# Attention backward with a period of eight half-steps, and a share of the base values made in the channel loop

## The chip, the core and the metric

The kernel runs on one core of one Trainium2 chip. The metric is the device time of one launch, in microseconds, median of several runs. A core has five engines with a queue each, and every queue is worked off in order: TensorE (PE, matrix products, results in PSUM), VectorE (DVE), ScalarE (ACT), GpSimd (POOL) and SyncE (SP, which here only issues transfers). They wait for one another through semaphores.

## What is computed

The launch computes a forward pass and all its gradients. The output mixes an attention block and a state-space block with a gate of one value for each token:

```python
g = _sigmoid((x * gate_w).sum(-1, keepdims=True))
a = _A_ref(x, A_wqkv, A_wo)          # 32 heads of width 18, 2048 tokens, width 576
b = _B_ref(x, B_A_re, ..., B_Dskip)  # a long convolution for each of 576 channels, 128 states
return g * a + (1 - g) * b
...
scores = jnp.einsum("bhqd,bhkd->bhqk", q, k) * (Dh ** -0.5)
p = _softmax(scores, axis=-1)
o = jnp.einsum("bhqk,bhkd->bhqd", p, v)
...
P = jnp.exp(logdA[:, :, None] * l[None, None, :])
K = jnp.einsum("dn,dnl,dn->dl", Cc, P, dB).real
```

`reference` returns the output and, by `jax.vjp`, the gradients of twelve inputs.

## The kernel before

The program has four stages. The first one (s1) projects x to q, k and v, makes the gradient of the attention's output and prepares parameters. The second one is the attention, forward and backward. The third (s4) loops over 18 blocks of 32 channels for the state-space part. The last one makes the weight gradients and the outputs. The change concerns the second and the third.

**Attention.** Heads are taken in 8 groups of four (`NG`), and each group's queries in 4 pieces of 512 tokens (`NQ`). A pair of group g and piece b is a *unit*; there are 32 (`NU`). The four heads of a group lie in four strips of 32 partitions, so that products over two heads run side by side in TensorE. A unit is worked off in 32 *half-steps* (`NST`), so 1024 in all (`NTOT`), and one loop over G runs through them with the order of every engine written out by hand (`manual_schedule`: nothing is reordered). In half-step G

- the forward part of half-step G makes the scores of two heads for 128 keys and 512 queries (`P1`, PSUM tile `ps` of tag S), and ScalarE their exponential `PT` (L802, 128x1024);
- the backward part runs 39 half-steps behind (`OFF`, G2 = G - 39). It makes the same scores the other way round (`P3`, tag S as well, exponential `eb`, L807) and the products of dO and V for two heads (`P2`, tag dP, two buffers of one bank). VectorE multiplies each of these with `PT` into `ds` (L812, 128x512), two for each half-step.

Tag S has two buffers of two banks, used in turn by P1 and P3, so P1 of the next half-step can be written only when the exponential of this P1 has been read. PSUM has one bank more for `accO` (the forward result) and one single bank of tag `accB`. Everything else shares `accB`, one after the other:

- V: eight products `accV<-eb,dOa` for the gradient of v (`dv_burst`, evicted by VectorE at L502 or L508);
- Q: eight products `accQ<-ds,Ktok` for the gradient of q (`dq_burst`, L523 or L528);
- K: sixteen half-width products `accK<-dsT,Qtok` for the gradient of k (`dk_half` twice, L554 or L556), which need `ds` transposed (`dsT`);
- F: once in a unit the transposition of the forward result (L411).

These bursts come with a period of four half-steps: V, Q, K and a fourth one, in which TensorE turns one head's part of `ds` (`turn_ds`, four 128x128 transpositions into `dst_p`, L463, copied by VectorE to `dsT`, L464). The other head parts are turned by transfers that SP issues (L820): of the eight head parts of a pair of key blocks, seven by transfer and one by TensorE, and all eight by transfer in one pair of eight (`by_pe`). `fill` puts products of two constant tiles into the bank ahead of the real ones; `NFILL` says how many: none for V and Q, one for K, three in the fourth half-step. A half-step's burst is called after the next half-step's P1 (`evs = late()`).

`post_forward` ends a unit's forward part: `f0` copies `accO` (L407); `f1` turns it and VectorE scales it (L416, L419), GpSimd makes `dOa` and `prod` (L421, L423); `f2` reduces `prod` (L429) and SP turns `dOa` into `dOaT`, which P2 of that unit reads.

**Base values.** The s4 stage needs for every channel a table E of powers (128 x 2 x 128). In the attention GpSimd, otherwise little used, makes it: 36 groups (`k`) of 16 channels, each with 28 small instructions that make powers and then 48 of 256 elements (`e_main`, L571: 32 products `et<-eG,eT` and 16 sums `Eo<-et,et`), and a store to memory for every four channels (`E_d<-Eo`, L619). `e_emit` spreads them over the half-steps by an estimate of their cost. GpSimd's queue also holds the packing of finished gradients (`pack`, L446 and L447, six half-steps after the transfer that turns them) and, at each unit's end, L421 and L423.

**The channel loop (s4).** For each block i: VectorE's recurrence (`scan`, 14 steps of L997, L1000, L1001), its products L1016, L1022, L1023, then `pairs1` and `pairs2` (L1067, L1095), all on two operands in SBUF. TensorE's products with `E1n` (loaded from `E_d` by `load_en`, six buffers) and with its transposed copy `E1e` stand around them. GpSimd has two small instructions for each block (`sums`, L1103 and L1104), which read `m4`, a copy that ScalarE makes into a single buffer (L1101).

Of the kernel before, what the change touches and what calls it, by code (L numbers as in the profile page):

```python
# [17 lines left out]
P = 128  # L18


def build(tc, aps, dbg_aps=None, stages=("s1", "attn", "post", "s4", "final")):
# [40 lines left out]
    with ExitStack() as gctx:  # L62
# [275 lines left out]
        x_v = x2.rearrange("(t p) d -> p t d", p=P)  # L338
        if "attn" in stages:
# [4 lines left out]
            NFILL = (0, 0, 1, 3)  # L344
            with ExitStack() as ctx:
                ctx.enter_context(tc.manual_schedule(engines={mybir.EngineType.PE, mybir.EngineType.Activation, mybir.EngineType.DVE, mybir.EngineType.Pool, mybir.EngineType.SP}))
                ga = ctx.enter_context(tc.tile_pool(name="ga", bufs=2))
                ptp = ctx.enter_context(tc.tile_pool(name="ptp", bufs=21))
# [39 lines left out]
                PB = {"QaT": 3, "VaT": 4, "Vtok": 5, "Ktok": 4, "Qtok": 2}  # L388
# [4 lines left out]
                def new_unit(g, b):  # L393
                    U = dict(PT={}, ds={}, eb={})
                    U["dO"] = work.tile([P, TPQ, 4, DH], BF, tag="dO", name="dO_b")
                    nc.sync.dma_start(U["dO"].rearrange("p t a b -> p t (a b)"),
                                      dO_d[:, b * TPQ:(b + 1) * TPQ, 4 * g * DH:4 * (g + 1) * DH])
                    U["dOa"] = dOa2[(g * NQ + b) % 2]
                    UN[(g, b)] = U

                def post_forward(g, b, acc):
# [7 lines left out]
                    def f1(po):  # L409
# [4 lines left out]
                        def ev():  # L414
# [7 lines left out]
                            prod = st["prod"] = work.tile([P, TPQ, 4, DH], F32, tag="prod", bufs=1, name="prod")  # L422
# [13 lines left out]
                def grad_tile():  # L436
                    return work.tile([P, KB], BF, tag="gb", bufs=3, name="gb")

                def store_grad(gb, g, which, t0):
                    c0 = which * D + g * 4 * DH  # L440
                    gT = work.tile([P, TPQ, 4, HP], BF, tag="gT", bufs=3, name="gT")
                    nc.sync.dma_start_transpose(out=gT.rearrange("p t a b -> p t (a b)"), in_=gb)

                    def pack():
                        dtk = work.tile([P, TPQ, 4, DH], BF, tag="dtk", bufs=2, name="dtk")
                        nc.gpsimd.tensor_copy(dtk, gT[:, :, :, 0:DH])  # L446
                        nc.gpsimd.dma_start(dqkv_d[:, t0:t0 + TPQ, c0:c0 + 4 * DH], dtk.rearrange("p t a b -> p t (a b)"))  # L447
                    packs.append((now[0] + 6, pack))
# [9 lines left out]

                def turn_ds(U, p):

                    pt_ = apsp.tile([P, TPQ, P], BF, tag="accB", name="dst_p")
                    for qb in range(TPQ):
                        nc.tensor.transpose(pt_[:, qb, :], U["ds"][2 * p + 1][:, 0, qb * P:(qb + 1) * P], ident_bf)  # L463
                    return lambda: nc.vector.tensor_copy(U["dsT", p][:, 1, 0:TPQ, :], pt_)  # L464

                def by_pe(g, b, p):
                    return ((g * NQ + b) * (NST // 4) + p) % 8 != 5

# [13 lines left out]
                ACC = []  # L482
# [7 lines left out]
                def dv_burst(g, b, kq, half):  # L490
                    U = UN[(g, b)]
                    acc = ACC.pop()
                    for n_ in range(2):
                        ii = 2 * half + n_
                        for j in range(4):
                            mm(acc[HP * j:HP * (j + 1), :], lhsT=U["dOa"][:, ii, j, :], rhs=U["eb"].pop((kq, ii, j)),
                               start=(n_ == 0), stop=(n_ == 1), tile_position=(0, HP * j))

                    def ev():
                        if b == 0 and half == 0:  # L500
# [3 lines left out]
                        a_ = DKV[("v", g, kq)]  # L504
                        o_ = a_
                        if b == NQ - 1 and half == 1:
                            o_ = DKV[("v", g, kq)] = grad_tile()
# [3 lines left out]
                def dq_burst(g, b, p):  # L511
                    U = UN[(g, b)]
                    acc = ACC.pop()
                    for n_ in range(2):
                        i = 2 * p + n_
                        for j in range(4):
                            mm(acc[HP * j:HP * (j + 1), :], lhsT=grp_t[g]["Ktok", i // TPQ][:, i % TPQ, HS * j:HS * j + HP], rhs=U["ds"][i][:, j, :],
                               start=(n_ == 0), stop=(n_ == 1), tile_position=(0, HP * j))

                    def ev():  # L520
                        if p == 0:
# [4 lines left out]
                        if p == NST // 4 - 1:  # L526
# [4 lines left out]
                def dk_half(g, b, p, h, st):  # L531
                    U = UN[(g, b)]
                    if h == 0:
                        st["acc"] = ACC.pop()
                    acc = st["acc"]
                    for qb in (2 * h, 2 * h + 1):
                        for j in range(4):
                            mm(acc[HP * j:HP * (j + 1), 0:2 * P].rearrange("p (a b) -> p a b", b=P), lhsT=grp_t[g]["Qtok", b][:, qb, HP * j:HP * (j + 1)],
                               rhs=U["dsT", p][:, :, j * TPQ + qb, :], start=(qb == 0), stop=(qb == 3), tile_position=(0, HP * j))
                    if h == 0:  # L540
                        return None
                    kq = p // 2
                    sl = slice((p % 2) * 2 * P, (p % 2 + 1) * 2 * P)

                    def ev():
                        if b == 0 and p % 2 == 0:
                            DKV[("k", g, kq)] = work.tile([P, KB], F32, tag="dkacc", bufs=4, name="dkacc")
                        a_ = o_ = DKV[("k", g, kq)]
                        if b == NQ - 1:
                            if p % 2 == 0:  # L550
                                DKV[("kb", g, kq)] = grad_tile()
                            o_ = DKV[("kb", g, kq)]
                        if b == 0:
                            nc.vector.tensor_copy(a_[:, sl], acc[:, 0:2 * P])  # L554
                        else:
                            nc.vector.tensor_tensor(o_[:, sl], a_[:, sl], acc[:, 0:2 * P], op=A.add)  # L556
                    return ev

                CE = 16
                EH = 4  # L560
                NA, NBT = P // 16, 16
                T_ = work.tile([P, 2, CE, NBT + 1], F32, tag="eT", bufs=1, name="eT")
                G_ = work.tile([P, 2, CE, NA], F32, tag="eG", bufs=1, name="eG")
                for t_ in (T_, G_):
                    nc.gpsimd.memset(t_[:, 0, :, 0], 1.0)
                    nc.gpsimd.memset(t_[:, 1, :, 0], 0.0)
                eops = []
                ez = {}

                def pl(out, a, b, op):  # L570
                    nc.gpsimd.tensor_tensor(out, a, b, op=op)  # L571

                def e_tmp(k):
                    return work.tile([P, 2 * P], F32, tag=f"et{k}", bufs=1, name=f"et{k}")

                def load_z(k):
                    ez[k] = work.tile([P, 2, CE], F32, tag="ez", bufs=2, name="ez")
                    nc.gpsimd.dma_start(ez[k], par_d[:, 12:14, k * CE:(k + 1) * CE])

                def emit_power(dst, src, lo, n, sq):  # L580

                    x = src[:, :, :, 1:1 + n]
                    st = []

                    def mul(ri):
                        w_ = e_tmp(ri)[:, 0:2 * CE * n].rearrange("p (r c m) -> p r c m", r=2, c=CE)
                        pl(w_, x, sq[:, ri].unsqueeze(1).unsqueeze(3).to_broadcast([P, 2, CE, n]), A.mult)
                        st.append(w_)
                    est = 0.21 + 2 * CE * n * 0.0018
                    eops.append((est, lambda: mul(0)))  # L590
                    eops.append((est, lambda: mul(1)))
                    est = 0.2 + CE * n * 0.002
                    eops.append((est, lambda: pl(dst[:, 0, :, lo:lo + n], st[0][:, 0], st[1][:, 1], A.subtract)))
                    eops.append((est, lambda: pl(dst[:, 1, :, lo:lo + n], st[0][:, 1], st[1][:, 0], A.add)))

                Eo = {}

                def e_main(k, c):
                    q = k * CE + c
                    for ri in range(2):  # L600
                        st = []

                        def mul(gi, ti, st):
                            if ti == gi == 0 and q % EH == 0:
                                Eo[q // EH] = work.tile([P, EH, 2, P], BF, tag="Eo", bufs=2, name="Eo")
                            w_ = e_tmp(gi)
                            pl(w_.rearrange("p (c a b) -> p c a b", c=2, b=NBT),
                               G_[:, gi, c:c + 2, :].unsqueeze(3).to_broadcast([P, 2, NA, NBT]),
                               T_[:, ti, c:c + 2, 0:NBT].unsqueeze(2).to_broadcast([P, 2, NA, NBT]), A.mult)
                            st.append(w_.rearrange("p (c l) -> p c l", c=2))  # L610

                        def add(ri, st):
                            o_ = Eo[q // EH][:, q % EH:q % EH + 2, ri, :]
                            if ri == 0:
# [827 lines left out]
```

## Time and profile before

| | us |
|---|---|
| median of 3 runs | 3099.37 (3094.06 to 3100.29) |
| profiled execution | 3094.2, span 3092.5 |
| s1 | 0 to 206 |
| attention, forward only (39 half-steps) | 206 to 248 |
| attention, both parts | 248 to 2219 |
| attention, backward only (the last 39 half-steps and their bursts) | 2219 to 2302 |
| s4: preparation and first blocks | 2302 to 2360 |
| s4: the rest of the loop | 2360 to 2880 |
| last stage | 2880 to 3092.5 |

The stages' borders are first and last starts of `PT`, `eb` and of the recurrence. The page's sums over the whole span put PE at 84% of it, DVE at 80%, ACT at 77% and POOL at 58%. No engine stands out there, and these shares are means over stages that differ: POOL is busy almost only in the attention. So the stages are read one by one.

### The profile page before, as it was taken

What the parts mean: (1) busy time and instruction counts of PE and PEld (TensorE: products, weight loads), DVE (VectorE), ACT (ScalarE), POOL (GpSimd) and SP (SyncE); (2) the same over time, 40 slices, a digit from 0 to 9 for tenths busy, and PEclk for the clock granted to TensorE, in tenths of its full rate; (3) what the DMA queues carried; (4) which work ended last, traced back from release to release, by engine and by line L of the source; (5) the groups of instructions that cost most, each with busy time, mean ns of one, the idle gap of its engine ahead of it and who ended that gap; (6) DMA issues with size and microseconds to landing.
All of it is one profiled execution on the core that took longest, in us unless ns stands there. A gap on an engine that the chain in (4) does not pass through costs nothing. (4 is left out here: it accounts for less than half of the span.)

```text
span 3092.5 us, 70491 instructions
## 1 busy us (share of the span) xinstructions
PE 2608.6 (84%) x27147; PEld 1202.5 (39%) x27147; DVE 2464.7 (80%) x4531; ACT 2395.3 (77%) x2765; POOL 1799.7 (58%) x3371
## 2 busy tenths in 40 slices
PE   4768999899899899889889989989866887786679
PEld 2432232232233233223223323323225777776347
DVE  4436898898899899889889989989964888888634
ACT  2458999999899899999899989989836677675111
POOL 0038888988888889888898888988110000000010
PEclk8878999999999899999999999999987888888789
DMA  8757999899989999989998998898788887772885
GB/s 221 154 142 129 173 165 180 156 168 166 163 166 164 170 163 165 178 158 167 164 165 163 172 171 159 167 172 162 133 151 243 213 208 204 206 200 79 228 205 132
DMA packets 1409063, 529.41 MB, mean 171 GB/s; under 512 B 1303487, under 2 KB 1378849, under 8 KB 1399509
## 3 DMA queue, kind: packets, MB, share of 16 engines
q1 hardware_dynamic: 1380212, 464.27, 78.5%
q0 software_dynamic: 20624, 53.26, 6.6%
q10 hardware_dynamic: 7888, 7.38, 0.8%
q8 instruction: 212, 3.47, 0.4%
q14 instruction: 127, 1.03, 0.1%
HBM read 144.48 MB, written 99.69 MB: 79 GB/s over the span
## 5 line engine op out<-in xcount | busy, mean ns | idle before, releaser
L812 DVE TENSOR_TENSOR ds<-ps_P,PT 128x512 bf16<-128x512 f32 x2048 | 1312.3, 681 | 18.5 <-PE ps_P L30 14.4
L807 ACT ACTIVATE eb<-ps_P 128x1024 bf16<-128x1024 f32 x1024 | 1058.1, 1033 | 125.1 <-PE ps_P L30 120.7
L802 ACT ACTIVATE PT<-ps_P 128x1024 bf16<-128x1024 f32 x1024 | 1058.7, 1037 | 41.1 <-PE ps_P L30 39.1
L571 POOL TENSOR_TENSOR et<-eG,eT 128x256 f32<-128x256 f32 x1152 | 700.1, 629 | 35.5
L30 PE MATMUL ps_P<-dOaT,VaT_g 32*128 32x512 bf16 x2048 | 561.9, 390 | 51.3 <-DVE ds L812 43.8
L30 PE MATMUL ps_P<-QaT_g,KaT_g 32*128 32x512 bf16 x2048 | 413.6, 398 | 124.7 <-ACT PT L802 110.0
L571 POOL TENSOR_TENSOR Eo<-et,et 128x256 bf16<-128x256 f32 x576 | 418.7, 727 | 42.4
L30 PE MATMUL ps_P<-KaT_g,QaT_g 32*128 32x512 bf16 x2048 | 406.2, 389 | 1.4 <-ACT eb L807 1.0
L1103 POOL TENSOR_TENSOR SS<-m 128x96 f32<-128x96 f32 x18 | 7.8, 431 | 556.9 <-ACT m L1101 556.9
L30 PEld LDWEIGHTS <-KaT_g 32*128 32x128 bf16 x2048 | 135.4, 92 | 432.7 <-issue 430.9
L30 PEld LDWEIGHTS <-QaT_g 32*128 32x128 bf16 x2048 | 114.9, 91 | 310.4 <-issue 288.3
L30 PE MATMUL accF<-ident_bf,J_bf 128*128 128x512 bf16 x783 | 225.8, 399 | 10.0 <-DVE gb L556 10.0
L30 PE MATMUL accO<-PT,Vtok_g 128*32 128x512 bf16 x2048 | 213.2, 403 | 0.0
L464 DVE COPY dsT<-dst_p 128x512 bf16<-128x512 bf16 x224 | 95.0, 424 | 111.0 <-PE dst_p L463 109.9
L30 PEld LDWEIGHTS <-J_bf 128*128 128x128 bf16 x1103 | 89.1, 100 | 226.3 <-issue 194.6
L30 PE MATMUL accK<-dsT,Qtok_g 128*32 128x256 bf16 x4096 | 166.0, 284 | 0.0
L30 PE MATMUL accQ<-ds,Ktok_g 128*32 128x512 bf16 x2048 | 158.9, 387 | 2.8 <-DVE gb L508 1.5
L30 PE MATMUL accV<-eb,dOa 128*32 128x512 bf16 x2048 | 159.0, 388 | 2.2 <-DVE dsT L464 1.6
L959 ACT COPY E1e<-etp 128x1024 bf16<-128x1024 bf16 x144 | 135.8, 1040 | 16.8 <-PE etp L958 16.8
L30 PE MATMUL yp<-Rw,E1n 128*128 128x30 bf16 x1152 | 67.7, 232 | 83.7 <-DVE Rw L1022 69.1
L30 PEld LDWEIGHTS <-E1n 128*128 128x128 bf16 x2304 | 96.7, 109 | 101.2 <-issue 100.7
L508 DVE TENSOR_TENSOR dvacc<-dvacc,accV 128x512 f32<-128x512 f32 x192 | 130.1, 678 | 0.1
(243 smaller groups left out, 3911.6 us busy)
## 6 DMA issues: line engine op xcount, KB each, us to landing
E_d<-Eo POOLq DMA_DIRECT2D x144, 256.0 KB, 3.9
E1n<-E_d SPq DMA_DIRECT2D x36, 1024.0 KB
xs<-xb_d SPq DMA_DIRECT2D x18, 1024.0 KB
T0w<-Kp_d SPq DMA_DIRECT2D x18, 1024.0 KB
Md_d<-mst SPq DMA_DIRECT2D x36, 288.0 KB
dsT<-ds SPq DMA_TRANSPOSE x512
dqkv_d<-dtk POOLq DMA_DIRECT2D x96, 72.0 KB, 4.4
QKV_d<-stg SPq DMA_DIRECT2D x12, 504.0 KB
```

Source lines behind the costliest of these rows:

```text
L30: return nc.tensor.matmul(out, lhsT=lhsT, rhs=rhs, start=start, stop=stop, **kw)
L464: return lambda: nc.vector.tensor_copy(U["dsT", p][:, 1, 0:TPQ, :], pt_)
L508: nc.vector.tensor_tensor(o_, a_, acc, op=A.add)
L571: nc.gpsimd.tensor_tensor(out, a, b, op=op)
L802: nc.scalar.activation(U["PT"][i][:, j:j + 2, :], ps, ACT.Exp)
L807: nc.scalar.activation(e, ps, ACT.Exp)
L812: nc.vector.tensor_tensor(U["ds"][i][:, j, :], ps, U["PT"][i][:, j, :], op=A.mult)
L959: nc.scalar.copy(E_[:, 4 * q:4 * q + 4], pt_)
L1103: nc.gpsimd.tensor_tensor(o_[:, :, 0], m4[:, :, 0], m4[:, :, 3], op=A.subtract)
```

## The change

- The bursts get a period of eight half-steps, set by `slot = (G2 + 1) % 8`: V in slots 0 and 1, Q in 2 and 3, K in 5 and 6. Two bursts now add up in the bank, and VectorE evicts once, after the second: 128x512 for V, Q and K alike. In slots 4 and 7 TensorE turns.
- A turn takes two head parts, the last head's of both key blocks of a pair (eight transpositions, one copy 128x2x512); one pair of eight is left to the transfers, the one whose slot F takes. Transfers turn three heads of each key block.
- `NFILL` becomes one fill for V and none elsewhere; the fourth half-step's three and K's one go.
- A burst is now issued in its own half-step, and V's second half comes one half-step after the last exponential that it reads. The heads of P2 and P3 are taken in another order, still in strips apart from each other.
- `PT` is held in 41 half tiles in place of 21 whole ones, `eb` has 8 buffers for 6, `ds` 5 for 4. Fewer: `Vtok` 4 for 5, `gb` and `gT` 2 for 3, `dtk` 1 for 2, `dO_b` 1 for 2 and loaded six half-steps later, `prod` shares a buffer with `oT`. Finished gradients are packed 4 half-steps after their transfer is issued.
- `basis_ops` makes the base values; groups 0 to 27 (`KE` = 28) stay in the attention, 28 to 35 are made in s4: `basis_share(i)` issues them in 15 equal shares from block -1 to block 13, ahead of `pairs2(i)` and `sums(i)` in the code, on GpSimd.
- `E1n` has 5 buffers for 6. The second half of block i+2 is loaded in the middle of block i; before, it was loaded with the first half, at the end of block i-1.

```diff
-            NFILL = (0, 0, 1, 3)
+            NFILL = {"V": 1, "Q": 0, "K": 0}
...
-                def by_pe(g, b, p):
-                    return ((g * NQ + b) * (NST // 4) + p) % 8 != 5
+                def by_pe(p):
+                    return 0 if p == NPF else NTURN
...
+                    n = by_pe(p)
+                    pt_ = apsp.tile([P, n, TPQ, P], BF, tag="accB", name="dst_p")
+                    for x in range(n):
+                        for qb in range(TPQ):
+                            nc.tensor.transpose(pt_[:, x, qb, :], U["ds"][2 * p + 2 - n + x][:, 3, qb * P:(qb + 1) * P], ident_bf)
+                    return lambda: nc.vector.tensor_copy(U["dsT", p][:, 2 - n:2, 3 * TPQ:, :], pt_)
+                NTURN, NPF = 2, 5
...
+                def dv_half(g, b, kq, h, acc):
+                    for ii in (2 * h, 2 * h + 1):
                         for j in range(4):
                             mm(acc[HP * j:HP * (j + 1), :], lhsT=U["dOa"][:, ii, j, :], rhs=U["eb"].pop((kq, ii, j)),
-                               start=(n_ == 0), stop=(n_ == 1), tile_position=(0, HP * j))
+                               start=(ii == 0), stop=(ii == 3), tile_position=(0, HP * j))
...
+                SLOTS = {0: ("V", dv_half, 0), 1: ("V", dv_half, 1), 2: ("Q", dq_half, 0), 3: ("Q", dq_half, 1), 5: ("K", dk_half, 0), 6: ("K", dk_half, 1)}
...
-                    evs = late()
+                    evs = []
+                    slot = (G2 + 1) % 8
+                    m_ = (G2 - (7, 8, 8, 8, 8, 8, 8, 0)[slot]) // 8
+                    if ("f1", G) in todo:
+                        acc = accB("accF")
+                        evs.append(todo.pop(("f1", G))[0](acc))
+                    elif 0 <= m_ < NTOT // 8:
...
+                            if h == 0:
+                                acc = accB("acc" + nm)
+                                fill(acc, NFILL[nm])
+                                burst(g, b, kq, 0, acc)
+                            else:
+                                evs.append(burst(g, b, kq, 1, acc))
...
+                        elif by_pe(2 * kq + (slot == 4)):
+                            evs.append(turn_ds(UN[(g, b)], 2 * kq + (slot == 4)))
...
-                for k in range(D // CE):
+            for k in range(k0, k1):
...
+                eops4, load_z4 = basis_ops(pw, KE, D // CE)
+                load_z4()
+                def basis_share(i):
+                    want = len(eops4) * min(1.0, (i + 2) / (NBLK - 3))
+                    while e4[0] < want:
+                        eops4[e4[0]][1]()
+                        e4[0] += 1
...
                         ybp(i, 0)
+                        if sb is not None:
+                            load_en(sb, 1)
                         ybp(i, 1)
...
-                        load_en(mb, 1)
...
+                    basis_share(i)
                     if cur:
                         pairs2(i)
                         sums(i)
```

## The prediction

> **What bounds the kernel now.** I read the busy sums by stage first, then the waits inside the long stage, then single half-steps, then the one place in s4 where GpSimd works. By stage (us; busy us and count of PE, its weight loads, DVE, ACT, POOL; granted clock, DMA share, GB/s):
>
> ```profile
> 206.00:248.20 42.20, 34.17 (x155) 7.86 (x155) 2.06 (x5) 37.77 (x40) 36.07 (x67) 0.50 0.18 41
> 248.20:2219.20 1971.00, 1789.54 (x17665) 589.56 (x17665) 1739.93 (x3066) 1840.56 (x1969) 1709.24 (x3185) 0.97 0.94 165
> 2219.20:2302.00 82.80, 65.97 (x624) 21.20 (x622) 72.71 (x131) 41.98 (x42) 11.79 (x20) 0.94 0.84 146
> 2360.00:2880.00 520.00, 401.53 (x6679) 380.77 (x6679) 446.83 (x912) 349.75 (x514) 15.72 (x36) 0.82 0.70 181
> ```
>
> In the attention four engines are busy 87 to 93%: none has the stage to itself, they hold each other up. In s4 DVE leads (447 of 520) and POOL does nothing. The waits between 300 and 2219 (total, times, longest, us) and ACT's and PE's timeline (start, us) over one period:
>
> ```profile
> PE ps_P L30 <- ACT PT L802: 98.2, 366, 0.5
> ACT eb L807 <- PE ps_P L30: 88.1, 232, 4.4
> DVE dsT L464 <- PE dst_p L463: 104.6, 207, 1.2
> DVE dl L429 <- POOL prod L423: 31.2, 12, 4.2
> ```
>
> ```profile
> 1230.89 1.04 ACT L802 ACTIVATE PT<-ps_P 128x1024 bf16<-128x1024 f32 x1
> 1231.79 1.06 ACT L807 ACTIVATE eb<-ps_P 128x1024 bf16<-128x1024 f32 x1
> 1232.69 1.07 ACT L802 ACTIVATE PT<-ps_P 128x1024 bf16<-128x1024 f32 x1
> 1234.59 1.02 ACT L802 ACTIVATE PT<-ps_P 128x1024 bf16<-128x1024 f32 x1
> 1235.83 1.02 ACT L807 ACTIVATE eb<-ps_P 128x1024 bf16<-128x1024 f32 x1 [0.22 <-PE ps_P L30]
> 1236.74 1.02 ACT L802 ACTIVATE PT<-ps_P 128x1024 bf16<-128x1024 f32 x1
> ...
> 1233.82 0.39 PE L30 MATMUL ps_P<-QaT_g,KaT_g 32*128 32x512 bf16 x2 [0.24 <-ACT PT L802]
> 1234.14 0.82 PE L30 MATMUL accF<-ident_bf,J_bf 128*128 128x512 bf16 x3
> 1235.02 0.38 PE L463 MATMUL dst_p<-ident_bf,ds 128*128 128x128 bf16 x4
> 1235.34 0.39 PE L30 MATMUL ps_P<-KaT_g,QaT_g 32*128 32x512 bf16 x2
> ```
>
> Unhindered exponentials start 0.90 us apart, so ACT's floor is 1.81 us a half-step, though each lasts 1.04. PT starts 1.80, 1.90, 2.15 apart, and 1.81 in the V half-step that follows: 7.66 for four, 1.915 each. The long one is the half-step with fills: between P1 (1233.82) and P3 (1235.34) PE does three fills (0.88) and four turns (0.32), and `eb` waits for P3. K's, with one fill (0.32) and 0.55 of products, loses 0.09. V and Q (0.59) lose nothing. Hence a burst of about 0.8 us hides under an exponential, and each 0.1 more costs 0.1.
>
> The stage needs 1971.0/984 = 2.003 a half-step, so 87 us are lost outside this pattern. They lie at unit ends, where `prod` is late on GpSimd (last wait above), and after each such stall the clock drops for 3.4 or 6.8 us.
>
> In s4 all DVE operands are in SBUF. POOL and DVE at the first `sums`:
>
> ```profile
> 2394.61 0.40 POOL L1103 TENSOR_TENSOR SS<-m 128x96 f32<-128x96 f32 x1 [88.12 <-ACT m L1101]
> 2394.98 0.45 POOL L1104 TENSOR_TENSOR SS<-m 128x96 f32<-128x96 f32 x1
> ...
> 2394.79 0.37 DVE L1001 TENSOR_TENSOR HG<-tz 128x128 f32<-128x128 f32 x1
> 2395.20 0.51 DVE L997 TENSOR_TENSOR tz<-HG,par 128x256 f32<-128x256 f32 x1
> 2395.74 0.29 DVE L1000 TENSOR_TENSOR tz<-tz,UV 128x128 f32<-128x128 f32 x1
> ```
>
> L1001 takes 0.29 alone (its median; the line after it, L1000, is back to its own 0.29) and 0.37 beside POOL, L997 0.43 and 0.51. Over the 17 such pairs that meet the recurrence, DVE's instructions took 3.55 us more than their medians for 15.0 us of POOL: 24%.
>
> [...]L1001 lay wholly beside POOL and lost 0.08, not 0.4. [...]
>
> **The change, part by part.**
>
> *Regular half-steps.* For eight: fills go from eight (six at 0.29, two at 0.32) to one, turns from eight to sixteen at 0.08. Bursts per slot become: V 0.91 with its fill; V again 0.59, but its last four products read an `eb` exponential from the half-step before, which ends some 0.3 after they could start, so about 0.89; Q 0.59 twice; turn 0.64; K 0.55 twice; turn 0.64. Only the two V slots pass 0.8: together 0.08 to 0.24, I take 0.16. Eight cost 8 x 1.81 + 0.16 = 14.64 against 15.32: 0.085 a half-step, over 984: **-84 us**.
>
> *DVE.* Evictions fall from 2.4 for V and Q and 0.7 for K to 1.8 (0.60 from start to start). A turn's copy doubles from 0.42[...]; I take 0.7. Per eight, DVE goes from 13.9 to about 13.2, 90% of 14.64. As ACT sets the pace this is worth nothing by itself. The 0.51 us wait for `dst_p` goes with the fills: turns end where `ds` ends.
>
> *Unit ends.* GpSimd is busy 1709 of 1971 there. A group of base values is 42.2 us (L571 1435.9 and L619 84.7 us, over 36), so eight are 338 us; what stays is 1371 of some 1840, 75%. The lateness of `prod` should go. Its packs come 4 half-steps after their transfer, with one `dtk`; the 25% of slack covers that. I leave 0.6 us a unit for F and 20 us for clock dips, 39 of the 87: **-48 us**.
>
> *Tail.* DVE is busy 72.7 of 82.8; with its fewer evictions and no fills: **-8 us**. The first half-steps start at clock 0.50[...]: **+5**.
>
> *Transfers.* `dsT` moves 50 head parts for 57 in a unit, so DMA (share 0.94) is not fuller at the faster pace. K's second half reads `dsT` six half-steps (11 us) after its issue, not seven; transfers issued at 1231.30 had moved by 1237, so nothing is due. SP's loads that move (`Vtok` two later, `dO_b` six later) are needed 18 and 28 half-steps on. Two `gb` for three may hold K's eviction in the last unit of a group, by 1 us at most: 0 to 30 us, I take 0.
>
> *s4.* Two of the 15 shares run before the recurrence, where DVE is idle; 13/15 of 338 = 293 us meet it, about 20 us a block of 29, so POOL stays within the block and `sums`, queued behind a share, comes in time. By time: 24% of 293 x 1.15 (POOL is slowed too) = 81 us. By element: 209 ns a pair for 192 elements, 1.09 ns; the shares have 99,200: 108 us, as these instructions stream more of their time. I take 100. Of DVE's own waits (28 us for `hR` between 2390 and 2850) some 20 take it up: **+80 us**. From below 45 (longer vectors hide it); from above 280, if each instruction locks the other out[...].
>
> *E1n.* The later half load is issued at `ybp`'s middle (2559, 2586) for products at 2569 and 2597: 10 us for 1 MB at some 200 GB/s, 5 us. Zero, thin; without it up to 2 us a block.
>
> Sum: -84 - 48 - 8 + 5 + 80 = **-55 us**: 3039 from the profiled 3094.2, and 3044 on the median, which is 5 above it.
>
> **The rivals.** *A, the sum:* 3044, own range 3000 to 3085. *B, sharing is cheap* (the low bound of s4, +35 to +45): 3005; L1000 beside POOL often kept 0.29. Against it: L1001 reached 0.50. *C, the lock:* +280 in s4 for +80 gives 3245; [...]the quoted lines against. *D, the clock (slower):* fills also kept PE active. [...] At half clock a half-step is PE's 2.85 in place of 1.83, 0.36 us lost for each. A holds some 60 us of half clock; D decides from 210 us (mean clock 0.945), and at 0.915 (some 310 us) gives 3135. Quiet stretches at 1.00 now and the doubled turns speak against it. *E, gains and sharing meet:* 3080 to 3115; own account for a slower F or turn copy.
>
> **How the numbers follow.** A 0.50, B 0.12, C 0.10, D 0.18, E 0.10. The bound of "same" is 0.2%, about what a measurement of this kernel tells from none. Faster: A but 0.01, B, 0.03 of E: 0.64. Same: 0.04 of E and 0.01 of A: 0.05. Slower: C, D, 0.03 of E: 0.31. The range holds A, B, E and most of D: 2990 to 3150.
>
> **What would show it.** Half-steps of 1.83 with `eb` waiting only in V slots; no `dl` wait for `prod`; the both-part attention near 1840 us at clock 0.97 or more; s4's L997 at 0.5 and L1001 at 0.38 in blocks to 13 and back to 0.43 and 0.29 after; the loop near 600 us. Wrong if the attention's clock falls below 0.945, if s4 grows by over 140, or if half-steps stay at 1.9.

## The result, and the profile after

The changed kernel takes 3130.49 us (median of four runs, 3121.43 to 3136.84), beside 3097.36 for the kernel before: a ratio of 1.0105 (95% interval 1.0071 to 1.0139). It is slower by 33 us, where the prediction said 55 us faster. The profiled execution took 3136.36 us with a span of 3134.7, and its span is 42 us longer than the span before. Most line numbers have moved by 29: `PT` is L773, `eb` L778, `ds` L783, the recurrence L968, L971 and L972. The turn's copy is now L556 (it was L464) and GpSimd's base values are L356 (L571).

First the sums by stage of the kernel after, with the columns used above: start only, both parts, tail, and the loop from the first recurrence of block 0 to that of block 14.

```profile
204.90:244.70 39.80, 32.99 (x152) 7.46 (x152) 2.06 (x5) 37.40 (x39) 26.18 (x50) 0.50 0.17 36
244.70:2139.10 1894.40, 1696.69 (x17655) 574.88 (x17655) 1649.52 (x2699) 1829.14 (x1970) 1372.53 (x2533) 0.94 0.88 153
2139.10:2222.00 82.90, 65.06 (x621) 21.52 (x620) 69.07 (x120) 41.81 (x42) 12.55 (x24) 0.77 0.75 136
2272.70:2810.50 537.80, 322.05 (x5410) 305.21 (x5411) 514.00 (x728) 295.57 (x428) 450.31 (x620) 0.76 0.64 172
```

The same 14 blocks in the kernel before:

```profile
2352.00:2763.20 411.20, 324.39 (x5362) 306.66 (x5363) 353.86 (x728) 290.92 (x425) 11.34 (x26) 0.83 0.80 206
```

The attention with both parts is 77 us shorter (1894.4 for 1971.0). The 14 blocks are 127 us longer, and VectorE alone is 160 us busier there (514.0 for 353.9). The rest, all small, comes to -8. So the loop took back more than the attention gained.

The waits inside the attention, from 300 to 2139 (total, times, longest, us; `rl` is the factor with which VectorE scales the forward result at a unit's end):

```profile
POOL dOa L507 <- DVE rl L502: 271.4, 30, 14.2
DVE ds L783 <- PE ps_P L30: 99.0, 142, 2.1
ACT eb L778 <- PE ps_P L30: 49.3, 97, 1.8
DVE dsT L556 <- PE dst_p L555: 2.0, 3, 0.7
```

GpSimd now stands waiting at every unit's end, 9 us each time: it is early where it was late, and no wait of `dl` for `prod` is left. The wait of the turn's copy has gone from 104.6 to 2.0. VectorE, with fewer evictions, now waits for P2's products (`ds`, 99.0 for 7.0 before). ACT's timeline over a stretch with the two V slots shows the pattern that was forecast:

```profile
683.35 1.15 ACT L773 ACTIVATE PT<-ps_P 128x1024 bf16<-128x1024 f32 x1
...
685.16 1.18 ACT L773 ACTIVATE PT<-ps_P 128x1024 bf16<-128x1024 f32 x1
687.10 1.08 ACT L773 ACTIVATE PT<-ps_P 128x1024 bf16<-128x1024 f32 x1
...
689.05 1.02 ACT L773 ACTIVATE PT<-ps_P 128x1024 bf16<-128x1024 f32 x1
```

`PT` starts 1.81 apart, then 1.94 and 1.95 in the V slots. Over the middle 16 half-steps of all units the median is 1.841, against 1.916 before. That is 74 us over 984 half-steps. What is lost outside the regular pattern (the stage's time less 984 regular half-steps) was 86 us and is 83: nothing was won there. In its place stands the clock. Between 250 and 2130 us the trace's record of the granted clock has 109 us at half speed before and 194 after (here and below without the first stretch at half speed, which begins ahead of the attention and reaches into it). I cut the stage into stretches of 32 half-steps with one unit's end in each and set their loss against their time at half clock: 13 stretches without any lose 0.56 us each, and every us at half clock goes with 0.305 us lost, which is 59 us for the 194. Such a fit doesn't say which of the two brings the other about. But in the middle of units, away from their ends, the half-steps that lie wholly at half clock take 2.43 us in the mean (42 of them) for 1.84: there each us at half clock loses 0.24. By this estimate 47 of the 59 us are the price of the clock itself.

In the loop the groups of instructions by form (count, total us, mean ns of one, idle before) show who pays:

```profile
L356 POOL TENSOR_TENSOR et<-eG,eT 128x256 f32<-128x256 f32 x232 | 193.2, 853 | 7.2
L968 DVE TENSOR_TENSOR tz<-HG,par 128x256 f32<-128x256 f32 x196 | 124.1, 633 | 6.7
...
L972 DVE TENSOR_TENSOR HG<-tz 128x128 f32<-128x128 f32 x196 | 103.7, 529 | 6.7
...
L1038 DVE TENSOR_TENSOR pq<-UV,hR 128x1920 bf16<-128x1920 bf16 x28 | 37.9, 1393 | 1.8 <-DVE Rw L994 0.5
```

The same groups before, the short recurrence and the long products:

```profile
L997 DVE TENSOR_TENSOR tz<-HG,par 128x256 f32<-128x256 f32 x196 | 84.3, 430 | 6.7
...
L1067 DVE TENSOR_TENSOR pq<-UV,hR 128x1920 bf16<-128x1920 bf16 x28 | 31.2, 1154 | 35.4 <-ACT hR L1008 34.7
```

L972 took 298 ns before, and GpSimd's product took 629 in the attention. All of them are slower beside one another. From block 14 on, where the shares are done, L968 is back at 428. VectorE's wait for `hR`, 34.7 us before, is gone from the list of waits: 160 - 35 = 125 of the 127 us.

### The profile page after: what moved, and what is told of

Read it like the earlier page. It is cut to its first block, busy times and chain, and to the rows that moved or that the text cites. A ratio compares the mean times of both kernels' runs of the same rounds, so it can differ in the third digit from the quotient of the medians.

```text
span 3134.7 us, 70484 instructions
## 1 busy us (share of the span) xinstructions
PE 2510.4 (80%) x27132; PEld 1184.0 (38%) x27132; DVE 2531.2 (81%) x4147; ACT 2387.1 (76%) x2765; POOL 1930.1 (62%) x3375
## 5 line engine op out<-in xcount | busy, mean ns | idle before, releaser
L783 DVE TENSOR_TENSOR ds<-ps_P,PT 128x512 bf16<-128x512 f32 x2048 | 1310.7, 682 | 151.3 <-PE ps_P L30 112.9
L778 ACT ACTIVATE eb<-ps_P 128x1024 bf16<-128x1024 f32 x1024 | 1094.1, 1069 | 84.0 <-PE ps_P L30 82.8
L773 ACT ACTIVATE PT<-ps_P 128x1024 bf16<-128x1024 f32 x1024 | 1095.5, 1072 | 13.3 <-PE ps_P L30 11.0
L356 POOL TENSOR_TENSOR et<-eG,eT 128x256 f32<-128x256 f32 x1152 | 752.9, 674 | 35.5
L30 PE MATMUL ps_P<-dOaT,VaT_g 32*128 32x512 bf16 x2048 | 586.2, 402 | 46.4 <-DVE ds L783 33.5
L30 PE MATMUL ps_P<-QaT_g,KaT_g 32*128 32x512 bf16 x2048 | 435.6, 407 | 139.8 <-ACT PT L773 124.6
L356 POOL TENSOR_TENSOR Eo<-et,et 128x256 bf16<-128x256 f32 x576 | 434.9, 755 | 42.8
L30 PE MATMUL accV<-eb,dOa 128*32 128x512 bf16 x2048 | 196.7, 419 | 26.9 <-ACT eb L778 25.2
L556 DVE COPY dsT<-dst_p 128x1024 bf16<-128x1024 bf16 x224 | 152.4, 680 | 4.8 <-PE dst_p L555 4.7
L968 DVE TENSOR_TENSOR tz<-HG,par 128x256 f32<-128x256 f32 x252 | 148.5, 589 | 8.6
L555 PE MATMUL dst_p<-ident_bf,ds 128*128 128x128 bf16 x1792 | 146.4, 228 | 9.4 <-DVE gb L612 6.6
L356 POOL TENSOR_TENSOR et<-eT 128x32 f32<-128x32 f32 (+3 forms) x288 | 134.8, 487 | 11.3
```

What stands on the lines that cost most here:

```text
L30: return nc.tensor.matmul(out, lhsT=lhsT, rhs=rhs, start=start, stop=stop, **kw)
L555: nc.tensor.transpose(pt_[:, x, qb, :], U["ds"][2 * p + 2 - n + x][:, 3, qb * P:(qb + 1) * P], ident_bf)
L556: return lambda: nc.vector.tensor_copy(U["dsT", p][:, 2 - n:2, 3 * TPQ:, :], pt_)
L773: nc.scalar.activation(U["PT"][i, j // 2], ps, ACT.Exp)
L778: nc.scalar.activation(e, ps, ACT.Exp)
L783: nc.vector.tensor_tensor(U["ds"][i][:, j, :], ps, U["PT"][i, j // 2][:, j % 2, :], op=A.mult)
```

## The experiments

Twelve kernels ran, each beside the kernel before on the same chip. Three questions were open: what sharing costs and why, what GpSimd's room is worth in the attention, and what the clock has to do with it. Figures for the attention run from the first to the last `eb` (2042 us before, 1964 after), those for the loop are the 14 blocks (411 and 538). The expectations add up the durations of VectorE's instructions in the blocks (362 us before, 521 after); the views count the time in which it is busy (353.9 and 514.0).

**all36: no sharing, all base values in the attention.**

```diff
-        KE = D // CE - 4 * (CB // CE)
+        KE = D // CE
...
-                    basis_share(i)
```

> The change with all 36 groups of base values back in the attention and none in the channel loop. The traces so far: the first 14 blocks of the loop took 411 us before and 538 after (+127), and VectorE's own busy time in them grew from 362 to 521. Theory 'sharing' (the 127 us are the price of making base values beside the recurrence, and the attention gains nothing from the room made on GpSimd): the 14 blocks are back at 411 to 416, the attention from first to last eb stays at 1964 +- 15, total 3130 - 127 = about 3003 (2990 to 3020). Rival 'room' (the attention needs that room: dOa and prod come late at unit ends again, as before the change): the 14 blocks are back, but the attention grows by 30 to 60, total 3035 to 3065, with waits of dl for prod of 30 us and more.

3062.94 us (ratio 0.9880, interval 0.9862 to 0.9898). The blocks are back at 406, so the 127 us are the price of sharing; the five buffers and later load of `E1n`, which are still there, cost nothing. But the attention grew by 64 us to 2028, and that is the rival, "room" (its waits of `dl` come to 27.5 us, a little under the 30 it named). The regular half-step is still 1.841; the loss outside it went from 83 to 144 us and half clock from 194 to 287. Its waits:

```profile
DVE dl L515 <- POOL prod L509: 27.5, 12, 4.1
PE accK L30 <- DMA dsT<-ds: 19.9, 9, 5.5
```

and SP's own queue:

```profile
SPq L528 <- POOL dtk L532: 49.4, 20, 6.6
```

The last line was 10.3 us in 11 times in the changed kernel and 1.7 in three before. A full GpSimd packs gradients late. With two `gT` buffers for three, SP then stands in front of the next gradient's transfer, and K's products wait for `dsT` transfers. That these queue up behind SP's wait is inferred from the two lines and was not tested; no run has a third `gT` buffer.

**before_share: the old attention with the loop's sharing.** The kernel before with `KE` = 28, `basis_share` and the change's loading of `E1n`.

> The kernel before with its own attention, but groups 28 to 35 made in the channel loop as in the change (with the change's loading of E1n). Theory 'sharing': the 14 blocks go from 411 to about 538, as in the change. Its attention has GpSimd less full; if the 31 us that dl waited for prod at unit ends, and the clock dips after them, came from GpSimd's load, the attention (2042 from first to last eb) falls by up to 48, total 3175 to 3225. Rival (those losses came from elsewhere, VectorE's extra work at a unit's end): attention within 10 of 2042, total 3215 to 3230. Rival for the loop (the +127 came with the faster attention, not with the sharing): blocks grow by less than 80.

3200.34 us (1.0325, 1.0297 to 1.0352). The blocks took 538 us: sharing costs the same with either attention. The attention fell by 8 us only (2034), as its rival said (within 10 of 2042), though the total lies below the 3215 that the rival named. `dl` no longer waits for `prod`, yet 79 us are still lost outside the regular pattern (86 before): TensorE now waits for the transfer `dOaT` in its place, 26 us in seven times, where it was 2.3. So the lateness of `prod` was worth next to nothing in the old attention, and this is the step "the lateness should go: -48" taken alone. Why that transfer is late was not followed further.

**before_nofill: the old attention without fills.**

```diff
-            NFILL = (0, 0, 1, 3)
+            NFILL = (0, 0, 0, 0)
```

> The kernel before with no fills at all and nothing else changed. Of its regular half-steps 1.916 us, the change's 1.841. Theory 'fills' (the whole gain of the regular half-step is the fills taken out; the period of eight adds nothing to it): regular half-step 1.81 to 1.84, and half clock in the attention rises from 109 us to 200 to 300, which gives back 30 to 60 of the 75 to 100 us: total 3035 to 3075. Rival 'period' (one eviction per two bursts is needed for it): regular half-step 1.88 or more, total 3080 or more.

3100.84 us (1.0006, 0.9987 to 1.0025): no change. The regular half-step fell to 1.815, below the change's own, so the fills were what made it 1.916. But the whole gain of 99 us was given back, and in the profiled execution more. The sums of this run's attention with both parts (its profiled execution, 3119.9 us, is the longest of its runs):

```profile
247.00:2241.50 1994.50, 1743.64 (x16676) 569.13 (x16676) 1752.47 (x3066) 1847.16 (x1970) 1709.04 (x3185) 0.83 0.93 163
```

The granted clock is 0.83 where it was 0.97. Half clock went from 109 to 607 us, no stretch of 32 half-steps is free of it, and the loss outside the regular pattern rose from 86 to 209 us at 0.339 us for each us. "Theory fills" had the half-step right and put half clock at less than half of what came, so its total was missed too. So it is not the period of eight that makes the half-step short. The new attention runs almost without fills at far less half clock: 287 us with GpSimd as full as here (all36) and 194 in the change, for 607. Which part of it keeps the clock up, the doubled turns, the joined bursts or the one fill that V keeps, was not separated.

**unit_fill and half_fill: fills put back into the change,** near unit ends only, or of half width in every period.

```diff
+                        fill(acc, 2)                      # unit_fill, ahead of F
...
+                            if G2 % NST == NST - 2:       # unit_fill, ahead of one turn
+                                fill(accB("accX"), 1)
...
+                                if nm != "V":             # half_fill, Q and K
+                                    fill(acc, 1, w=2)
+                            fill(accB("accX"), 1, w=2)    # half_fill, ahead of turns
```

> The change with fills only near each unit's end: two before the F transpositions, one more before K's and V's first halves and one for K's second half (two of half width) and one before the turn, once in a unit. In the change's attention some 200 us run at half clock, nearly all of it in the first ten half-steps after a unit's end. Theory 'clock' (TensorE's low activity in these half-steps lets the clock fall): half clock in the attention falls below 100 us, the attention by 25 to 45, total 3085 to 3105. Rival 'VectorE' (F's extra VectorE work, about 2 us in three half-steps, stalls TensorE, and the clock only follows; fills then come behind the same stalls): half clock stays at 150 to 220 us, time unchanged or up to 12 longer (3125 to 3142).

> The change with one fill of half width (0.15 us) in Q's and K's first half, K's second half and both turns of every period, where the bursts are 0.55 to 0.64 us and so stay below the 0.8 that hides. In the change, units of 32 half-steps without a clock dip lose 0.56 us against the regular pace, and each us at half clock costs 0.305: 59 of the 80 us lost go with 194 us at half clock. Theory 'clock': half clock falls below 100 us, the regular half-step stays at 1.84, the attention shrinks by 25 to 45 us, total 3085 to 3105. Rival 'VectorE' (the dips follow stalls that fills don't cure): half clock 150 to 220, time as the change, 3125 to 3135. Third, the fills are not hidden: regular half-step 1.87 and more, 30 us longer.

unit_fill took 3137.33 us (1.0120, 1.0099 to 1.0140) and half_fill 3156.87 (1.0170, 1.0139 to 1.0201). Half clock fell from 194 us to 78 and 99, as "clock" said. The time did not follow. Stretches without half clock now lose 1.18 and 1.05 us in place of 0.56, and half_fill's regular half-step is 1.858, near the third of its expectations (fills that are not hidden). unit_fill's attention is 14 us shorter, less than the 25 to 45 of "clock"; in its profiled execution parts that the edit does not touch (the first stage, the loop, the last stage) came out 11 us longer together, so nothing of it shows in the total. half_fill's attention is 14 us longer. Half of the extra time of half_fill's median is not located: its profiled run is only 15 us above the change's. So the clock answers to fills, but of the 59 us neither of these runs saved more than 14 in the attention, as the fills cost time themselves.

**gated32 and share32: half the work in the loop, behind the recurrence or where it falls.** Both keep 32 groups in the attention. gated32 holds each share back:

```diff
+                    if i >= 0 and e4[0] < len(eops4):
+                        gate_t = pw.tile([P, 1], F32, tag="gate_t", name="gate_t")
+                        nc.gpsimd.tensor_copy(gate_t, blk(i)["HG"][:, 0, NS - 1, 0:1])
```

> The change with four groups of base values in the channel loop for eight (32 in the attention), and each block's share held back by a one-element copy on GpSimd that reads the last column of the recurrence, so that it runs beside the nine long VectorE instructions behind the recurrence and not beside the 42 short ones. Theory 'each instruction' (a VectorE instruction beside GpSimd loses about 0.22 us whatever its length: in the change 0.30 to 0.53, 0.43 to 0.63, 1.15 to 1.42, 2.15 to 2.40): 9 x 0.25 x 14 = 32 us more VectorE time, most of it taken from the 35 us that VectorE waited for hR; the 14 blocks take 411 to 430, and with the attention at 1964 to 1990 the total is 3000 to 3045. Rival 'in proportion' (VectorE loses 36% of the time GpSimd works, 159 of 441 us in the change): 169 us of work, slowed to about 200, cost 72 us, less 30 from the waits: 14 blocks of 450 to 460.

> As gated32 (four groups in the channel loop), without holding the shares back behind the recurrence. gated32's 14 blocks took 468 us (411 before), and the products behind the recurrence went from 1.15 to 1.51: more than a fixed 0.25 each. Theory 'in proportion' (VectorE loses about 0.53 us for each us of GpSimd's work as it would be undisturbed, wherever it falls; 159/293 in the change, 82/157 in gated32): 455 to 475, total 3045 to 3070. Rival 'each instruction' (short ones are hit hardest): 14 blocks of 490 and more, total 3080 and more.

gated32: 3064.84 us (0.9877, 0.9856 to 0.9899), blocks 468. share32: 3068.05 us (0.9895, 0.9867 to 0.9923), blocks 464. The first theory fell with gated32, whose blocks are longer than its rival's 450 to 460 too; share32 is where "in proportion" put it. From the groups by form, gated32's short recurrence and long products:

```profile
L968 DVE TENSOR_TENSOR tz<-HG,par 128x256 f32<-128x256 f32 x196 | 101.3, 517 | 6.7
...
L1038 DVE TENSOR_TENSOR pq<-UV,hR 128x1920 bf16<-128x1920 bf16 x28 | 41.2, 1510 | 10.5 <-ACT hR L979 9.4
```

and share32's:

```profile
L968 DVE TENSOR_TENSOR tz<-HG,par 128x256 f32<-128x256 f32 x196 | 112.1, 572 | 6.7
...
L1038 DVE TENSOR_TENSOR pq<-UV,hR 128x1920 bf16<-128x1920 bf16 x28 | 31.2, 1155 | 8.3 <-ACT hR L979 6.7 <-DVE Rw L994 0.5
```

In share32 the loss falls on the recurrence alone and the long products keep their 1155. In gated32 these lose 0.36 each, more than the fixed 0.25, and the shares, slowed, still run on into the next recurrence. VectorE's busy time is 435.5 and 433.4 us, against 353.9 without sharing. Per us of GpSimd's work as it would be undisturbed (42.2 us a group) that is 82/158 = 0.52, 80/146 = 0.54, and 160/293 = 0.55 in the change: one price, whatever it meets. (gated32's blocks meet 14 shares of 15, the two others 13. Counting the shares' instructions inside the 14 blocks one by one, at the durations they have in the attention, gives 0.53 in all three.) The time of the blocks grows by less than VectorE's busy time, as its waits for `hR` take up a part.

**share_set and share_copy: the same instructions with no operand, and with one.** These leave the shares where the change has them, and leave out the base values that the shares would have made.

```diff
+                if wr:                                    # in the loop's shares alone
+                    nc.gpsimd.memset(out, 0.0)            # share_set
+                    nc.gpsimd.tensor_copy(out, a)         # share_copy
+                    return
                 nc.gpsimd.tensor_tensor(out, a, b, op=op)
```

> The change with the shares' products and sums in the channel loop replaced by GpSimd instructions that only write a constant to the same tiles, as many of them (this leaves out the base values of the last 128 channels). In the change VectorE lost 159 us to 293 us of GpSimd's work. Theory 'operands' (what costs is that GpSimd reads two operands from SBUF beside VectorE): VectorE loses less than 0.15 us for each us of these writes, 14 blocks of 411 to 420. Rival 'any work of GpSimd': 0.5 us for each us, so with some 130 to 200 us of writes 60 to 100 us of loss and blocks of 440 to 480.

> As share_set, with the shares' products and sums replaced by copies of their first operand, so that GpSimd reads one operand from SBUF (this leaves out the base values of the last 128 channels). In share_set VectorE's busy time in the 14 blocks was 362.5 us, as before the change (361.9), beside 150 us of writes; with two operands it was 521. Theory 'two operands' (only GpSimd instructions with two operands from SBUF hold VectorE up): 362 to 370, 14 blocks of 405 to 412. Rival 'reads' (each operand read costs): half of the 159 us, 430 to 450, 14 blocks of 440 to 470.

share_set: 3007.34 us, blocks 407. share_copy: 3035.14 us, blocks 424 (two runs each). The writes' recurrence and GpSimd groups:

```profile
L971 DVE TENSOR_TENSOR tz<-HG,par 128x256 f32<-128x256 f32 x196 | 85.2, 434 | 6.7
L357 POOL MEMSET et<- 128x256 f32 x238 | 68.5, 322 | 0.0
```

and the copies':

```profile
L357 POOL COPY et<-eG 128x256 f32<-128x256 f32 x221 | 144.7, 681 | 1.7
L971 DVE TENSOR_TENSOR tz<-HG,par 128x256 f32<-128x256 f32 x196 | 93.5, 477 | 6.7
```

GpSimd was busy 142 us with writes and VectorE lost nothing (354.4 us busy, 353.9 before). With one operand, 336 us of GpSimd's time cost VectorE 41 us; with two, 450 cost 160. So, with as many instructions in the same places, it was reading operands from SBUF that cost, and the second operand cost most. The three kinds also differ in length (0.32, 0.68 and 0.85 us for the large ones), but per us of GpSimd's busy time the order stays: nothing, 0.12, 0.36. Of share_copy's expectations neither holds: the loss lies between them.

**late36, late36_fill and late36b: room without sharing.** All 36 groups in the attention, but spread over its tail as well, where GpSimd had been idle.

```diff
-                    want = e_total * min(1.0, max(0.0, (G - 10) / (NTOT - 40)))
+                    want = e_total * min(1.0, max(0.0, (G - 10) / (NTOT + OFF + 10)))   # late36
+                    want = e_total * min(1.0, max(0.0, (G - 10) / (NTOT + 28)))         # late36b
```

> As all36 (no sharing in the channel loop), but the 36 groups are spread over the attention and its tail, to half-step 1083 in place of 994; GpSimd had nothing to do for 135 us there. From first to last eb the attention took 1964 us with 28 groups, 1971 with 32, 2028 with 36; at the slower rate it holds as many groups in a half-step as with 33. Theory 'room' (what decides is how full GpSimd is before each unit's end): attention 1970 to 1985, dl waits for prod below 10 us in total, total 3005 to 3025. Rival 'interference' (base values cost the attention something for each of them, wherever the queue stands): attention 2015 to 2030, total 3045 to 3065.

> late36 and half_fill together. Theories 'room' and 'clock' both right: 2970 to 2995; only 'room': 3005 to 3025; only 'clock': 3015 to 3040; neither: 3045 and more.

> As late36, but the 36 groups end at half-step 1062 in place of 1083. In late36 GpSimd's last base values ended 45 us after the last eb and the stretch from the last eb to the first recurrence grew from 63 to 92 us. The rate is now that of 33.7 groups. Theory 'room': attention 1972 to 1990, that stretch 63 to 72, total 3010 to 3030. Rival (the stretch is long for another reason, or the attention goes steeply between 33 and 34 groups): 3035 and more.

late36: 3038.99 us (0.9798, 0.9772 to 0.9824). The attention is 1972, as "room" said, but the total is above its 3025, as the stretch from the last `eb` to the first recurrence grew from 63 to 92 us: GpSimd's last base values ended 45 us after the last `eb`, and the next stage's first load stood waiting 47 us. late36b ends them earlier, and that goes: 3018.37 us (0.9745, 0.9721 to 0.9768), the attention 1969, the stretch 68, the blocks 406. That is the total that "room" gave it. late36_fill, with half_fill's fills, took 3062.22 us (0.9877, 0.9857 to 0.9897), 23 more than late36: here fills only cost. late36b beats both kernels, the one before by 2.5%.

## Why the prediction was wrong

The forecast of 3044 us and its sign were wrong. Its steps, from the profiled executions:

| step | put at, us | measured, us |
|---|---|---|
| regular half-steps | -84 | -74 |
| unit ends | -48 | -3 |
| tail, to the first recurrence | -8 | +1 |
| start | +5 | -2 |
| s4, the 14 blocks | +80 | +127 |
| elsewhere | 0 | -7 |
| sum | -55 | +42 |

*Regular half-steps.* The mechanism was right. The V slots take 1.95 and are the only long ones; they cost 0.25 in eight half-steps, where 0.16 was taken. The turn's copy took 0.68 (0.7 estimated), and it hides.

*s4: the term that turned the sign, mis-sized by 47 us.* The mechanism was right: both engines go on beside each other, each slower. The size came from 17 pairs of short `sums`. There VectorE lost 24% of GpSimd's time, and GpSimd was taken to be slowed by 1.15. The runs show 36% (160/450) and a slowing of about 1.5 (439 us, without `sums`, for 293), so VectorE lost 160 where 100 was taken: 0.55 us for each undisturbed us of GpSimd. By element it is 1.61 ns where 1.09 was taken. The 35 us of `hR` waits took up more than the 20 assumed, and the rest fell on the time. The lock of rival C did not come: by estimate, a lock over whole instructions would have cost VectorE about all of GpSimd's 293 us, and it lost 160. Why the short `sums` were the cheaper ones was not tested; the weak point of the argument was to carry their average over to long streams.

*Unit ends: the step that failed.* "The lateness of `prod` should go" was true, and "-48" did not follow. It counted a wait that something else takes over: in before_share the lateness went too, and only 7 us came back. In the changed kernel it is the clock that takes over: "20 us for clock dips" was 59, too low by a factor of three, while the 0.6 us a unit left for F agrees with the 0.56 that a stretch without half clock loses.

*The clock, rival D.* Its mechanism was right: fills held the clock up (in the old attention 109 us at half clock with them, 607 without). How busy TensorE must be for the clock to stay up no run shows. The price of 0.36 us for each us at half clock was an estimate, from a half-step of 2.85 us there (2.43 in the middle of units); the fit gave 0.305 (0.339 in before_nofill). The rival was put as all or nothing, deciding from 210 us (mean clock 0.945) with 60 in the main case. The whole stage, its first stretch at half speed included, came in at 212 us and a mean clock of 0.944, so this sign of being wrong was just met. The clock took what the unit ends should have given; it did not make the change slower by itself. The two errors, 45 us at the unit ends and 47 in s4, carry the whole miss, and their sum, 92, is near the 97 between -55 and +42. The tail's gain may have gone the same way, which was not tested: VectorE is less busy there (69.1 for 72.7), but the clock was 0.77 for 0.94. The +5 at the start was an estimate too: that stretch ran at clock 0.50 in both kernels and came out 2 us shorter.

*What sharing bought.* The prediction set GpSimd's room down as a gain over the kernel before. The runs show it as what the new attention needs to gain at all: with GpSimd full its attention is 14 us shorter than before, with room 78. The room was worth 64 us, and sharing it out cost 127. Giving it in the tail (late36b) cost some 10: 5 in the attention and 5 in the stretch behind it.

## What to carry to other kernels

Price work put beside another engine from the same kind of instruction at the same length and density, not from a few short ones; here every undisturbed us of GpSimd instructions with two operands from SBUF cost VectorE 0.52 to 0.55 us of busy time, wherever in the loop it lay, and only VectorE's own waits (35 us for `hR`) could hide a part of that. Look first for a stretch in which that engine is idle and the work costs the others little: spreading the same work over the attention's tail gave 3018 us where the loop gave 3130. And before taking out products that seem to do nothing, ask what TensorE's clock would do without them: taking out the fills alone won 99 us in the pattern, and the clock took all of it back.

## What the runs showed of the hardware

- GpSimd's loss depended on what it met, VectorE's did not: a product of 629 ns took 679 beside the short recurrence in share32, 1037 mostly beside the long products in gated32, and VectorE lost 0.54 and 0.52 us for each undisturbed us of GpSimd's work.
- GpSimd writing constants to SBUF cost VectorE nothing (142 us of writes, 0.5 us lost), and as many instructions that read one operand cost a quarter of those that read two (41 against 160 us).
- Without fills the attention ran 607 of 1880 us at half clock, with them 109, and the launch took the same time (3100.84 and 3098.81 us).
